# Two decode layers on one core: the whole first W_q kept in SBUF, a shorter ring, and a layer's first queries and scores head by head

## The chip, the cores and the metric

One Trainium2 chip, one of its cores. The metric is the device time of one execution of the program in microseconds. Before the change the median of three runs is 736.22 us (736.16 to 736.47).

## What is computed

Four sequences (B = 4) decode one token through two equal layers, each an attention block and a gated MLP with a residual around either. All arrays are float32. Both layers use the same weights and the same cache, of which the last W = 1024 positions count.

```python
def _A_ref(x, k_cache, v_cache, wq, wo):            # D = 640, 32 heads of 128, W = 1024
    q = (x @ wq).reshape(B, Sq, Hq, Dh).transpose(0, 2, 1, 3)
    k = k_cache[:, :, Sk - W:, :]; v = v_cache[:, :, Sk - W:, :]
    p = softmax(einsum("bhqd,bhkd->bhqk", q, k) * Dh ** -0.5)
    return einsum("bhqk,bhkd->bhqd", p, v).transpose(0, 2, 1, 3).reshape(B, Sq, Hq * Dh) @ wo

def _B_ref(x, W_gate, W_up, W_down):                # F = 1728
    gate = x @ W_gate
    return (gate * (gate > 0) * (x @ W_up)) @ W_down

x = x + _A_ref(layernorm(x), ...); x = x + _B_ref(layernorm(x), ...)   # twice
```

## The kernel before

All that is loaded lies in three arrays of 128 partitions, cut along the free axis. `heads` holds W_q, keys, values and W_o of heads 0 to 26 in the order in which layer 0 uses them. `kept` holds the same for heads 27 to 31, and the MLP's weights are `mlp`. A head's keys are 4096 floats per partition, its values another 4096 and its W_o 640; W_q of a group of four heads is 2560. Heads are taken in groups: 0 to 5 have four heads each and 6 has three, all of them in `heads`; 7 (K0) has three and 8 (K1) two, and these are the kept ones. In layer 0 the order is all groups in turn; in layer 1 the kept groups come first, from what is still in SBUF.

Nearly all of SBUF is one tile, `store`, of 53888 floats per partition. Loads go into it as a ring: `load` walks through a list `todo` of pieces and puts each at the place `at`, which then moves on by the piece's length and goes back to 0 at the end. A piece of `kept` has a fixed place instead, its own offset in its row: W_o at 0 to 3200, the queries of the kept groups at 3200 to 6400, then keys and values up to 47360 (`FRONT`). While these stay, from the end of layer 0's attention through its MLP, the ring is what is left of the store, 47360 to 53888, 6528 floats. `jumps` sets the place where a new stretch begins.

`load` is called while the program is written, after each product that has read its operand for the last time (`done`), and emits a load only when the places that it overwrites have been read. So the order of all loads is fixed, all of them stand on SP's queue one behind the other, and each waits there for the PE instruction that read its place last. A piece longer than 16384 ends where a quarter of the store ends. The first `HELD` = 1024 floats of `heads`, a part of W_q of group 0, are loaded once into a tile of their own, `first_q`, and serve both layers.

On PE, a group goes through `query` (5 chunks of W_q), `query_out` (scaling, on DVE), `query_turned` (transposes), `scores` (8 products of 512 columns per head: two halves of the positions for each of four sequences), `softmax`, `turned`, `values` (8 products of 512 columns per head) and `project`. The products with the values of a group come after the scores of the next one. A product in float32 is two PE instructions in the profile, and one row entry in the order of instructions shown further down. In `attention` the first two groups' queries are computed ahead of the first group's scores. In `forward`, `gate` multiplies by W_gate and W_up, `down` by W_down, 640 floats of it at a time; `busy` issues transposes into `po` whose results nobody reads. All schedules are written by hand: each engine takes its instructions in the order in which the code emits them.

Of the kernel before, what the change touches and what calls it, by code (L numbers as in the profile page):

```python
# [7 lines left out]
F32 = mybir.dt.float32  # L8
AF = mybir.ActivationFunctionType
ALU = mybir.AluOpType  # L10
# [3 lines left out]
P = 128  # L14
# [13 lines left out]
SIDE = 4  # L28
# [5 lines left out]
def of(what, g):  # L34
    return [(what, h) for h in HEADS[g]]


def step(g):
# [7 lines left out]
    "kept": [*of("o", K0), *of("o", K1), ("q", K0), ("q", K1), *of("k", K0), *of("k", K1), *of("v", K0), *of("v", K1)],  # L46
# [44 lines left out]
def decode_kernel(ctx: ExitStack, tc: tile.TileContext, x, source, sel, out):  # L91
# [3 lines left out]
    small = ctx.enter_context(tc.tile_pool(name="small", bufs=2))  # L95
# [6 lines left out]
    big.tile([P, 8], F32, name="pad")  # L102
# [37 lines left out]
    pieces(1, "heads", HELD, 2560, 3584, k, *range(k + 1536, k + 4 * 1536 + 1, 1536))  # L140
# [16 lines left out]
    def load(part=False):  # L157
# [4 lines left out]
        while todo:  # L162
# [69 lines left out]
    qT = const.tile([P, SIDE - 1 + SIDE * SIDE * B], F32, name="qT")  # L232
# [9 lines left out]
    eps_sb = const.tile([P, 1], F32, name="eps_sb")  # L242
# [28 lines left out]
    def normalized():  # L271
# [3 lines left out]
        su = small.tile([P, 1], F32, name="su", bufs=1)  # L275
# [5 lines left out]
        ss = small.tile([P, 1], F32, name="ss", bufs=1)  # L281
        nc.scalar.activation(sq, xc, AF.Square, accum_out=ss)
        busy(1)

# [6 lines left out]
        return ss  # L291

    def deviation(ss):
        var = mean(ss, "var")
        rs = small.tile([P, 1], F32, name="rstd")
        nc.scalar.activation(rs, var, AF.Sqrt, bias=eps_sb)
        nc.vector.reciprocal(rs, rs)
        return rs

    def table(func):  # L300

        t = small.tile([P, 1], F32, name="t", bufs=1)
        nc.scalar.activation(t, eps_sb, func)
# [7 lines left out]
    def query(layer, g, spread=False):  # L311


        n = len(HEADS[g]) * P
        qp[g] = ps_m.tile([P, n], F32, tag="m", name="qp")
        for c in range(KC - 1):
            nc.tensor.matmul(qp[g][32 * c:32 * c + 32, :], xT[:, B * c:B * c + 32], part(layer, "q", g, c * n, n),  # L317
                             start=True, stop=c > 0 and not spread, tile_position=(0, 32 * c))
        c = KC - 1
        m = n // 4 if spread else n  # L320
        for a in range(n // m):
            nc.tensor.matmul(qp[g][32 * a:32 * a + 32, a * m:a * m + m], xT[:, B * c:B * c + 32],  # L322
                             part(layer, "q", g, c * n + a * m, m), start=False, stop=True, tile_position=(0, 32 * a))
        part_done(layer, "q", g, 0, KC * n)

    def query_out(g, rstd):
        nc.vector.tensor_scalar(gates[:, :len(HEADS[g]) * P], qp.pop(g), rstd, SCALE, op0=ALU.mult, op1=ALU.mult)  # L327

    def query_turned(g):

        n = len(HEADS[g])
        qt = ps_m.tile([P, n, P], F32, tag="m", name="qt")
        for i in range(n):
            nc.tensor.transpose(qt[:, i], gates[:, i * P:(i + 1) * P], ident)  # L334

        at = qT[:, SIDE - 1:].rearrange("p (i b x) -> p i b x", i=SIDE, b=B)[:, :n, :, 0]
        nc.vector.tensor_reduce(at, qt.rearrange("p i (a x) -> p i x a", a=4)[:, :, :B], axis=AX.X, op=ALU.add)

    def scores(layer, g):
        n = len(HEADS[g])  # L340
        for i, h in enumerate(HEADS[g]):
            for j in range(2):
                for b in range(B):
                    lo = (j * B + b) * 512
                    at = SIDE - 1 + SIDE * (B * i + b) - i
                    nc.tensor.matmul(ps[32 * b:32 * b + SIDE, j, :], qT[:, at:at + SIDE], part(layer, "k", h, lo, 512),  # L346
                                     start=i == 0, stop=i == n - 1, tile_position=(0, 32 * b))
                    part_done(layer, "k", h, lo, 512)
        nm[g] = small.tile([P, 1], F32, name="nm")
        nc.vector.tensor_reduce(nm[g], ps.rearrange("p j n -> p (j n)"), axis=AX.X, op=ALU.max, negate=True)  # L350

    def softmax(g):
        sums[g] = small.tile([P, 1], F32, name="sm")
        nc.scalar.activation(probs, ps.rearrange("p j n -> p (j n)"), AF.Exp, bias=nm.pop(g), accum_out=sums[g])  # L354
# [28 lines left out]
    def totals(g):  # L383
        so = ps_m.tile([P, P], F32, tag="m", name="so")
        nc.tensor.transpose(so, sums.pop(g).to_broadcast([P, P]), ident)  # L385
        r[g] = small.tile([P, SIDE, B], F32, name="r")
        nc.vector.reciprocal(r[g], so.rearrange("p (b i) -> p i b", b=B)[:, :SIDE])  # L387

    def values_turned(g):
# [5 lines left out]
        oT[g] = small.tile([P, SIDE, B], F32, name="oT")  # L395
# [12 lines left out]
    def attention(layer):  # L408
        gs = order[layer]
        load(True)  # L410
        rstd = deviation(normalized())
# [34 lines left out]
    def forward(layer):  # L446
        load(True)
        ss = normalized()
# [26 lines left out]
        def hidden(j, h):  # L475
            hTs[j] = small.tile([P, 4, B], F32, name="hT", bufs=4)
# [11 lines left out]
        def down(j, last=False):  # L488
            for f in range(4 if j < 3 else 1):
# [6 lines left out]
                if not (last and f > 1):  # L496
                    busy(1)
# [10 lines left out]
        rstd = deviation(ss)  # L508
# [75 lines left out]
```

## Time and profile before

| | us |
|---|---|
| median of three runs | 736.22 (736.16 to 736.47) |
| the profiled execution | 736.33 |
| its span, first to last instruction | 734.46 |
| PE busy | 452.5 |
| DVE busy | 75.0 |
| ACT busy | 47.1 |
| HBM read | 312.24 MB |

The profile is of one execution. Its page lists busy times, and behind it stand views in the order of time: an engine's instructions, SP's issues and, for each load, the time from its issue to its landing. A product of 128 partitions by 512 columns has a long time of its own in a row's mean (700 ns), but four of them run side by side in different columns of the array, so a stretch of them is read from its start and its length. Rows of one line, engine and shape are merged with an "x" and their number.

### The profile page before, as it was taken

The numbers are of one execution on the slowest core, as the hardware profiler recorded it, in microseconds if no ns is written. First come the engines' busy times: TensorE is split into PE (matmuls) and PEld (weight loads), VectorE is DVE, ScalarE is ACT, GpSimd is POOL, SyncE is SP. The second block draws the span as 40 slices with busy tenths as digits, with TensorE's granted clock in tenths as the row PEclk, the third lists the DMA queues.
The fourth block names the chain that finished last, engine by engine and source line by source line (L and its number), as shares of the span: only waits on it lengthen the run. The fifth ranks groups of instructions, "written<-read, shape, count | busy, mean of one in ns | idle before, by whom it ended". The sixth has DMA issues, their size and how long they took to land.

```text
span 734.5 us, 8243 instructions
## 1 busy us (share of the span) xinstructions
PE 452.5 (62%) x3749; PEld 142.7 (19%) x3749; DVE 75.0 (10%) x279; ACT 47.1 (6%) x88; POOL 0.2 (0%) x4
## 2 busy tenths in 40 slices
PE   1657366555566635727789897446756545656686
PEld 0111111111121201202233231101211111122242
DVE  1011010010000101101101221001010100001010
ACT  1100000000000000000101110000000000000110
POOL 0000000000000000000000000000000000000000
PEclk9989787867678887969899999867878977668897
DMA  9999999999999999999999999999999999999996
GB/s 380 454 421 430 452 430 422 429 446 434 417 444 445 408 446 419 438 433 419 419 405 406 432 433 431 445 432 443 431 427 425 447 432 424 435 445 429 420 427 285
DMA packets 15738, 312.85 MB, mean 426 GB/s; under 512 B 1748, under 2 KB 2132, under 8 KB 7512
## 3 DMA queue, kind: packets, MB, share of 16 engines
q1 hardware_dynamic: 15552, 312.24, 99.1%
q8 instruction: 29, 0.48, 0.2%
q10 hardware_dynamic: 152, 0.09, 0.1%
q14 instruction: 5, 0.04, 0.0%
HBM read 312.24 MB, written 0.08 MB: 425 GB/s over the span
## 4 chain that ended last, share of the span: by engine, by line
DMA 54%; PE 30%; another core or an unknown queue 14%; issue 1%; DVE 1%; ACT 0%; SPq 0%; DVEq 0%; ACTq 0%
DMA store<-in_heads 32%; PE ps L346 12%; DMA store<-in_mlp 12%; DMA store<-in_kept 10%; PE po L374 9%; PE y L404 1%; PE qp L317 1%; PE pp L359 1%; PE qp L322 1%; PE gu L458 1%; PE qt L334 1%; PE ot L394 0%; PE po L259 0%; PE y L493 0%
## 5 line engine op out<-in xcount | busy, mean ns | idle before, releaser
L346 PE MATMUL ps<-store,qT 128*4 128x512 f32 x1024 | 160.9, 700 | 108.2 <-DMA store<-in_heads 104.3
L374 PE MATMUL po<-store,pT 128*16 128x512 f32 x1024 | 155.2, 718 | 105.4 <-DMA store<-in_heads 95.4
L374 PEld LDWEIGHTS po<-store,pT 128*16 128x16 f32 x1024 | 35.0, 110 | 210.8 <-issue 128.3
L346 PEld LDWEIGHTS ps<-store,qT 128*4 128x4 f32 x1024 | 29.4, 94 | 221.6 <-DMA store<-in_heads 119.9
L350 DVE TENSOR_REDUCE nm<-ps 128x1 f32<-128x1024 f32 x18 | 22.0, 1224 | 245.0 <-PE ps L346 245.0
L354 ACT ACTIVATE probs<-ps,nm 128x1024 f32<-128x1024 f32 x18 | 20.1, 1114 | 353.6 <-DVE nm L350 345.9
L317 PE MATMUL qp<-store,xT 128*32 128x512 f32 (+2 forms) x136 | 22.9, 614 | 24.7 <-DMA store<-in_heads 24.6
L404 PE MATMUL y<-store,oT 128*4 128x160 f32 x512 | 26.2, 335 | 8.7 <-DMA store<-in_heads 7.6
L458 PE MATMUL gu<-store,xT 128*32 128x256 f32 (+1 forms) x300 | 26.3, 414 | 8.3 <-DMA store<-in_mlp 7.9
L370 DVE COPY pT<-pp 128x16 f32<-128x16 f32 x128 | 17.1, 168 | 135.3 <-PE po L374 135.3
L381 ACT COPY gates<-po 128x512 f32<-128x512 f32 x16 | 9.4, 587 | 243.1 <-PE po L374 243.1
L359 PE MATMUL pp<-sel_sb,probs 128*128 128x128 f32 x144 | 19.5, 281 | 0.0
L322 PE MATMUL qp<-store,xT 128*32 128x512 f32 (+4 forms) x48 | 17.7, 514 | 0.0
L327 DVE TENSOR_SCALAR gates<-qp,rstd 128x512 f32<-128x512 f32 (+2 forms) x18 | 12.4, 691 | 48.4 <-PE qp L322 44.4
L359 PEld LDWEIGHTS pp<-sel_sb,probs 128*128 128x128 f32 x144 | 17.1, 146 | 0.0
L404 PEld LDWEIGHTS y<-store,oT 128*4 128x4 f32 x512 | 13.3, 93 | 19.5 <-DMA store<-in_heads 8.0
L387 DVE RECIPROCAL r<-so 128x16 f32<-128x16 f32 x18 | 4.6, 257 | 121.4 <-PE so L385 121.4
L458 PEld LDWEIGHTS gu<-store,xT 128*32 128x32 f32 x300 | 11.4, 123 | 18.9 <-issue 8.7
L394 PE MATMUL ot<-sel_sb,gates 128*128 128x128 f32 x72 | 11.7, 283 | 1.2 <-DVE gates L378 1.2
L334 PE MATMUL qt<-sel_sb,gates 128*128 128x128 f32 x64 | 12.3, 316 | 0.0
L493 PE MATMUL y<-store,hT 128*4 128x160 f32 x208 | 10.6, 305 | 1.7 <-DMA store<-in_mlp 1.7
L334 PEld LDWEIGHTS qt<-sel_sb,gates 128*128 128x128 f32 x64 | 7.6, 155 | 18.8 <-issue 17.5
(62 smaller groups left out, 107.2 us busy)
## 6 DMA issues: line engine op xcount, KB each, us to landing
store<-in_heads SPq DMA_DIRECT2D x18, 6656.0 KB, 54.0
store<-in_heads SPq DMA_DIRECT2D x7, 6912.0 KB, 52.0
store<-in_heads SPq DMA_DIRECT2D x2, 6592.0 KB, 54.4
store<-in_heads SPq DMA_DIRECT2D x2, 5376.0 KB, 65.4
store<-in_mlp SPq DMA_DIRECT2D x16, 640.0 KB, 6.9
store<-in_kept SPq DMA_DIRECT2D x4, 2048.0 KB, 39.9
store<-in_heads SPq DMA_DIRECT2D x3, 2560.0 KB, 22.0
store<-in_heads SPq DMA_DIRECT2D x1, 6896.0 KB, 46.1
```

The lines of the kernel that those rows point to most:

```text
L317: nc.tensor.matmul(qp[g][32 * c:32 * c + 32, :], xT[:, B * c:B * c + 32], part(layer, "q", g, c * n, n), start=True, stop=c > 0 and not sp ...
L322: nc.tensor.matmul(qp[g][32 * a:32 * a + 32, a * m:a * m + m], xT[:, B * c:B * c + 32], part(layer, "q", g, c * n + a * m, m), start=False ...
L327: nc.vector.tensor_scalar(gates[:, :len(HEADS[g]) * P], qp.pop(g), rstd, SCALE, op0=ALU.mult, op1=ALU.mult)
L334: nc.tensor.transpose(qt[:, i], gates[:, i * P:(i + 1) * P], ident)
L346: nc.tensor.matmul(ps[32 * b:32 * b + SIDE, j, :], qT[:, at:at + SIDE], part(layer, "k", h, lo, 512), start=i == 0, stop=i == n - 1, tile_ ...
L350: nc.vector.tensor_reduce(nm[g], ps.rearrange("p j n -> p (j n)"), axis=AX.X, op=ALU.max, negate=True)
L354: nc.scalar.activation(probs, ps.rearrange("p j n -> p (j n)"), AF.Exp, bias=nm.pop(g), accum_out=sums[g])
L359: nc.tensor.transpose(pps[g][c // 4][:, c % 4, :], probs[:, c * P:(c + 1) * P], ident)
L370: nc.vector.tensor_copy(to[:, 4 * j:4 * j + 4], pp[j][:, :, i:P:32])
L374: nc.tensor.matmul(po[32 * a:32 * a + SIDE * B, :], t[:, at:at + SIDE * B], part(layer, "v", h, c * 512, 512), start=i == 0 and c < 4, sto ...
L404: nc.tensor.matmul(y[32 * a:32 * a + B], o[:, i], part(layer, "o", h, a * QUARTER, QUARTER), start=False, stop=last and h == HEADS[g][-1], ...
L458: nc.tensor.matmul(gus[j][32 * g:32 * g + 32, :2 * n], xT[:, B * c:B * c + 32], get(layer, "mlp", lo, 2 * n), start=c == 0, stop=c == KC - ...
```

## The change

Six things are changed. The whole W_q of group 0 (`HELD` = 2560) is kept in `first_q`. The store shrinks to 52480 floats, so the ring beside the kept rows has 5120. A quarter's end is now at multiples of 13312. The queries of the two kept groups change places in `kept`, and layer 1's first loads go to `LATER` (4480), from where the first kept group's queries and its keys follow each other. In `attention` the first group's queries are multiplied head by head (`query_by_heads`), its scores too, and the second group's queries come behind them. In `down`, two unread transposes stand behind every second block of W_down in place of one behind each. Small tiles that had buffers of their own now lie in spare columns of `qT`'s buffer or share one pool.

```diff
-    "kept": [*of("o", K0), *of("o", K1), ("q", K0), ("q", K1), *of("k", K0), ...
+    "kept": [*of("o", K0), *of("o", K1), ("q", K1), ("q", K0), *of("k", K0), ...
...
-HELD = 1024
-STORE = 53888
-QUARTERS = [STORE // 4, STORE // 2, STORE // 4 * 3, STORE]
+HELD = KC * 4 * P
+STORE = 55040 - HELD
+QUARTERS = [13312, 2 * 13312, 3 * 13312, STORE]
 FRONT = KEPT * 2 * (D + KV)
-FIRST, FIRST_MLP = 10944, 53248
+LATER = (KEPT + len(HEADS[K1])) * D
+FIRST, FIRST_MLP = 10752, STORE - 640
...
-    pieces(1, "heads", HELD, 2560, 3584, k, *range(k + 1536, k + 4 * 1536 + 1, 1536))
+    pieces(1, "heads", HELD, 3584, k, *range(k + 1536, k + 4 * 1536 + 1, 1536))
...
-                at = FRONT if layer == 0 and row == "mlp" else KEPT * D if layer == 1 and spare else 0
+                at = FRONT if layer == 0 and row == "mlp" else LATER if layer == 1 and spare else 0
...
+    def query_by_heads(layer, g):
+        n = len(HEADS[g]) * P
+        qp[g] = ps_m.tile([P, n], F32, tag="m", name="qp")
+        for i in range(len(HEADS[g])):
+            for c in range(KC):
+                a = c if c < 4 else i
+                nc.tensor.matmul(qp[g][32 * a:32 * a + 32, i * P:i * P + P], xT[:, B * c:B * c + 32],
+                                 part(layer, "q", g, c * n + i * P, P), start=c < 4, stop=c != i, tile_position=(0, 32 * a))
+        part_done(layer, "q", g, 0, KC * n)
...
-        query(layer, gs[0], True)
-        query_out(gs[0], rstd)
-        query(layer, gs[1])
-        query_turned(gs[0])
-        go_on()
-        query_out(gs[1], rstd)
-        scores(layer, gs[0])
-        softmax(gs[0])
+        g, n = gs[0], len(HEADS[gs[0]])
+        query_by_heads(layer, g)
+        query_out(g, rstd, 0, 1)
+        query_out(g, rstd, 1, 2)
+        query_turned(g, 0, 1)
+        query_out(g, rstd, 2, n)
+        go_on()
+        head_scores(layer, g, 0)
+        query_turned(g, 1, n)
+        for i in range(1, n):
+            head_scores(layer, g, i)
+        query(layer, gs[1])
+        highest(g)
+        query_out(gs[1], rstd)
+        softmax(g)
         query_turned(gs[1])
...
-                if not (last and f > 1):
-                    busy(1)
+                if j == 3 or f == 1 or f == 3 and not last:
+                    busy(2)
```

Since the ring is shorter and begins elsewhere, the pieces end at other floats and lie at other places. Around layer 0's turn to the kept rows the lists read so (floats of the row, places in the store, and the last read that frees them). Keys of head 24, the first behind the turn, begin at float 207744 of `heads`; values of head 19 fill 203648 to 207744, in 8 blocks of 512.

| before | place | behind | after | place | behind |
|---|---|---|---|---|---|
| heads 191360 to 204672 | 40320 to 53632 | keys of head 19 | heads 188288 to 200576 | 39808 to 52096 | keys of head 19 |
| heads 204672 to 207744 | 0 to 3072 | W_o of head 11 | heads 200576 to 207744 | 0 to 7168 | values of head 12 |
| kept 3200 to 6400 | 3200 to 6400 | values of head 12 | kept 3200 to 6400 | 3200 to 6400 | 7th value block of head 19 |
| heads 207744 to 214400 | 6400 to 13056 | values of head 14 | heads 207744 to 214400 | 6400 to 13056 | 8th value block of head 19 |
| heads 214400 to 228224 | 13056 to 26880 | keys of head 21 | heads 214400 to 227712 | 13056 to 26368 | (long read) |
| heads 228224 to 238976 | 26880 to 37632 | keys of head 23 | heads 227712 to 238976 | 26368 to 37632 | (long read) |

On SP these are the following rows, first before the change, with the semaphores on which each waits. DMAHW names the semaphores of earlier loads, PE that of PE's instructions.

```order
L186 DMA store<-in_heads 128x13312 [waits PE_49]
L186 DMA store<-in_heads 128x3072 [waits DMAHW0_49,PE_49]
L186 DMA store<-in_kept 128x3200 [waits PE_49]
L186 DMA store<-in_heads 128x6656 [waits PE_49]
L186 DMA store<-in_heads 128x13824 [waits DMAHW2_49,DMAHW1_49,PE_49]
L186 DMA store<-in_heads 128x10752 [waits PE_49]
```

The same place of SP's queue after the change:

```order
L187 DMA store<-in_heads 128x12288 [waits DMAHW7_49,PE_49]
L187 DMA store<-in_heads 128x7168 [waits DMAHW0_49,PE_49]
L187 DMA store<-in_kept 128x3200 [waits DMAHW4_49,PE_49]
L187 DMA store<-in_heads 128x6656 [waits PE_49]
L187 DMA store<-in_heads 128x13312 [waits DMAHW1_49]
L187 DMA store<-in_heads 128x11264 [waits DMAHW2_49]
```

The last piece ahead of the kept queries has 7168 floats where it had 3072, and the two long pieces behind them no longer wait for PE themselves.

The second place is PE's order where layer 1 begins: from the layer norm's variance to the second group's turned queries, before the change.

```order
L268 MATMUL var<-ss,sel_sb 32x1 x4
L317 MATMUL qp<-store,xT 32x384 x4
L322 MATMUL qp<-store,xT 32x96 x4
L317 MATMUL qp<-store,xT 32x256 x4
L322 MATMUL qp<-store,xT 32x256
L334 MATMUL qt<-sel_sb,gates 128x128 x3
L307 MATMUL y<-probs,sel_sb 128x160
L346 MATMUL ps<-store,qT 4x512 x24
L334 MATMUL qt<-sel_sb,gates 128x128 x2
```

And after it:

```order
L273 MATMUL var<-qT,sel_sb 32x1 x4
L329 MATMUL qp<-store,xT 32x128 x15
L342 MATMUL qt<-sel_sb,gates 128x128
L308 MATMUL y<-probs,sel_sb 128x160
L353 MATMUL ps<-store,qT 4x512 x8
L342 MATMUL qt<-sel_sb,gates 128x128 x2
L353 MATMUL ps<-store,qT 4x512 x16
L318 MATMUL qp<-store,xT 32x256 x5
L342 MATMUL qt<-sel_sb,gates 128x128 x2
```

The first group's queries are 15 short products instead of 8 longer ones, the first head's scores stand ahead of the turning of the other two heads, and the second group's queries have moved behind all scores of the first.

More of the change, by code (lines that the diff above doesn't have):

```diff
@@ L309, in decode_kernel, with query @@
     qp, nm, sums, pps, r, oT = {}, {}, {}, {}, {}, {}
-    def query(layer, g, spread=False):
+    def query(layer, g):
         n = len(HEADS[g]) * P
         qp[g] = ps_m.tile([P, n], F32, tag="m", name="qp")
[L316 to L323, printed above, removed]
-        part_done(layer, "q", g, 0, KC * n)
@@ L339, in scores @@
-    def scores(layer, g):
[L340 to L349, printed above, removed]
+        for c in range(KC):
+            a = c % 4
+            nc.tensor.matmul(qp[g][32 * a:32 * a + 32, :], xT[:, B * c:B * c + 32], part(layer, "q", g, c * n, n),
+                             start=c < 4, stop=a > 0 or c == 4, tile_position=(0, 32 * a))
@@ L447, in forward @@
         load(True)
-        ss = normalized()
+        normalized()
         gus, hTs = {}, {}
```

70 lines of the change are left out of this document (44 added, 26 removed).

## The prediction

> **What bounds the kernel now.** First the page: its busy shares, its DMA queues, and then the busy time by stretch. In the second fence the columns are engine busy times, the granted clock, the busy share of the 16 DMA engines and what they moved.
>
> ```profile
> span 734.5 us, 8243 instructions
> PE 452.5 (62%) x3749; PEld 142.7 (19%) x3749; DVE 75.0 (10%) x279; ACT 47.1 (6%) x88; POOL 0.2 (0%) x4
> q1 hardware_dynamic: 15552, 312.24, 99.1%
> HBM read 312.24 MB, written 0.08 MB: 425 GB/s over the span
> ```
>
> ```profile
> 12.00:250.00 238.00, 136.41 (x986) 37.98 (x990) 21.83 (x74) 13.32 (x23) 0.00 (x0) 0.80 1.00 432
> 366.00:392.00 26.00, 22.45 (x256) 9.29 (x256) 2.09 (x10) 1.97 (x7) 0.00 (x0) 1.00 1.02 404
> 396.00:450.00 54.00, 49.89 (x483) 16.87 (x482) 12.01 (x34) 7.25 (x14) 0.00 (x0) 1.00 1.02 430
> 725.00:734.00 9.00, 5.47 (x114) 2.44 (x113) 0.93 (x4) 0.15 (x1) 0.00 (x0) 0.88 0.43 169
> ```
>
> The transfers are the bound: SP's queue keeps 16 engines busy for 99.1% of the span, at 432 GB/s with large pieces and 404 GB/s in layer 0's MLP with small ones, and no stretch before the last 9 us shows a gap. PE is busy for 62%, but for 49.89 of 54 us where layer 1 begins. Two things follow. A microsecond of transfer saved is a microsecond off the end. And a microsecond in which the queue is empty is lost, because nothing later has slack to win it back. So I ask of every part whether it takes bytes away, and whether SP ever has to wait until everything issued has landed.
>
> **The change part by part. Bytes.** W_q of head group 0 stays in SBUF whole, so layer 1 loads 1,536 floats per partition fewer: 1,536 x 512 B = 0.786 MB, at 432 GB/s **1.8 us less**. SP also issues two pieces fewer (the rows of its order: 105 against 107 loads through SP). A 640 KB piece is 0.655 MB, 1.62 us at 404 GB/s and 1.52 at 432, so an issue costs about 0.1 us: **0.2 us less**.
>
> **The turn to the kept rows in layer 0.** This is where I expect the time. Before, SP issues the queries of the kept heads early:
>
> ```profile
> 204.01 0.33 SPq L186 DMA_DIRECT2D store<-in_heads  x1
> 205.71 0.33 SPq L186 DMA_DIRECT2D store<-in_kept  x1
> 208.30 30.07 SPq L186 DMA_DIRECT2D store<-in_heads  x3
> store<-in_kept SPq DMA_DIRECT2D x1, 1600.0 KB, 48.4
> ```
>
> That piece is issued at 205.71 and lands 48.4 us later: 48 us of transfers lie ahead of it. Its place is fixed, 3200 to 6400. In the table of the change the piece of `heads` in front of it ended at place 3072; now it ends at 7168, and covers 3200 to 6400 with the values of head 19 from float 128 to 3328. The kept queries can start only when PE has read the seventh of head 19's eight blocks, and those blocks are in the piece issued immediately ahead. SP takes its queue in order, so behind this wait stand 6,656, 13,312 and 11,264 floats of `heads`; the order's rows show that the last two wait for no PE instruction of their own. So the queue runs dry: the piece lands, PE multiplies, and only then the next transfer starts. PE's rows there (start, length):
>
> ```profile
> 238.41 1.27 PE L404 MATMUL y<-store,oT 128*4 128x160 f32 x32
> 246.83 9.32 PE L374 MATMUL po<-store,pT 128*16 128x512 f32 x64 [7.15 <-DMA store<-in_heads]
> 262.01 5.10 PE L346 MATMUL ps<-store,qT 128*4 128x512 f32 x26 [2.90 <-DMA store<-in_heads]
> 119.54 8.09 PE po L374 x44
> 68.71 6.19 PE po L374 x52
> out_x<-probs SPq DMA_DIRECT2D x1, 80.0 KB, 1.6
> first_q<-in_heads SPq DMA_DIRECT2D x1, 512.0 KB, 3.9
> ```
>
> When does the piece land? At 246.83 PE starts on the piece that ends at float 204,672. 3,072 floats more are 1.573 MB, 3.6 us: 250.4. The way back from 262.01 agrees: that wait ended when the 3,200 kept floats and the 6,656 of `heads` had landed, 5.05 MB or 11.7 us later, so 250.3. The bytes up to float 207,744 are the same in the change, so this moment stays. What has PE left then? The last piece holds 14 value blocks (6 of head 18, 8 of head 19). The piece ahead ends at 200,576, 4,096 floats or 4.9 us before 204,672, so it lands at about 241.9. After its last key block come the query turn, the projection (1.27 us) and 18 value blocks at 9.32/32 = 0.291 us (two instructions to a block), 5.2 us: PE is done at about 249.2 and waits. Then 13 blocks, **3.8 us**, until the kept queries may go. Bounds: 6.19/26 = 0.238 us a block gives 3.1, 8.09/22 = 0.368 gives 4.8.
>
> From that issue to a moving stream again costs what an issue into an empty queue takes beyond its bytes. Two rows bound it. The output's 80 KB took 1.6 us, 0.2 of it bytes: 1.4. The first load's 512 KB took 3.9 us, 1.2 of it bytes: 2.7, in the cold first microseconds. I take **1.5**, next to the output, which like this one goes out in a program long under way. Together the stream stands still for **5.3 us** (4.5 to 7.5). Late next are the keys of head 24, for which PE waits at 262.01 already, so all after them moves by as much.
>
> On this restart the Trainium skill's page "DMA: Bandwidth & Descriptors" (section "Anatomy of one DMA — SWDGE (gpsimd) path") fits a fixed cost of about 2.0 us to one transfer, for a path that this kernel does not use. By it the standstill would be 5.8 us and the time, as an estimate, 740.8. The rows, 1.4 and 2.7, lie on both sides of it.
>
> **The smaller ring.** In layer 0's MLP the ring has 5,120 floats instead of 6,528. The first of these rows is from 370 to 375 us, the second from 385 to 390:
>
> ```profile
> store<-in_mlp SPq DMA_DIRECT2D x3, 640.0 KB, 6.9
> store<-in_mlp SPq DMA_DIRECT2D x3, 640.0 KB, 5.9
> 371.25 2.23 PE L458 MATMUL gu<-store,xT 128*32 128x256 f32 x20 [0.49 <-DMA store<-in_mlp]
> ```
>
> One turn of the ring at 404 GB/s now takes 8.3 us (3.34 MB), and 6.5 in the change (2.62 MB). In a turn a piece lands, PE reads it, SP issues its successor and that lands: 1.6 us for its 640 KB and 1.4 to 2.7 beyond them. That leaves PE 2.2 to 3.5 us to read a piece; 20 instructions, two pieces, took 2.23. So the 6.9 and 5.9 us were mostly queue, the turn still closes, and I put the MLP at **nothing**. It is tighter where layer 1 begins, since between the last W_down block and the first queries PE frees no place:
>
> ```profile
> 396.94 0.39 SPq L186 DMA_DIRECT2D store<-in_heads  x1
> store<-in_heads SPq DMA_DIRECT2D x1, 256.0 KB, 7.0
> 398.76 0.85 PE L317 MATMUL qp<-store,xT 128*32 128x384 f32 x8
> 399.66 6.61 SPq L186 DMA_DIRECT2D store<-in_heads  x6
> 401.40 5.33 PE L346 MATMUL ps<-store,qT 128*4 128x512 f32 x48
> 366.70 1.18 PE L458 MATMUL gu<-store,xT 128*32 128x128 f32 x27 [0.30 <-DVE xT L290]
> ```
>
> The piece issued at 396.94 lands 7.0 us later, at 403.9, and is the last one until 399.66, when the queries of group 7, layer 1's first, are read: 4.2 us of transfers lie ahead. In the change the ring holds 1,408 floats less, 1.7 us at 430 GB/s, so it would be empty at 402.2. The queries by heads are 15 products, 30 instructions; of that form 27 took 1.18, so 1.3 us against 1.0 now, and the issue comes at about 400.0, 2.2 us ahead: enough. It frees only 512 floats, 0.6 us, so the queue lasts to 402.8. The next piece waits for the first key block. One head's queries are copied and turned sooner than three, which about pays for the longer product, so the scores start as now at 401.4; four blocks run side by side in 4 x 0.22 us (48 instructions, 24 blocks, in 5.33), so its release is near 402.2. At 1.5 us beyond the bytes the stream resumes 0.9 us late. After that each block frees its place in 0.22 us and is refilled in 0.6, so nothing more is lost. **0.8 us** (0 if the first block is free at its own end, 2.0 at 2.7 beyond the bytes).
>
> **The rest costs nothing.** Head by head adds 7 products to group 7's queries and 12 to group 0's; the second queries come after the scores; the products that nobody reads are one more in number, in pairs. All of it is PE work, and what hides it is the transfers: elsewhere PE waits for them, as the rows of waits above show. The places where PE sets SP's pace are costed already. Without that cover the query's extra instructions would cost 0.3 us. The small tiles that move into one buffer change no row that I can price.
>
> **The sum.** The profiled execution took 736.3 us, 1.8 outside its span of 734.5; the median of the three runs is 736.2, so nothing is lost by starting there. 736.2 - 1.8 - 0.2 + 5.3 + 0.8 = **740.3 us**. With every bound low it is 736.2 - 2.0 + 4.5 + 0 = 738.7, with every bound high 736.2 - 1.8 + 7.5 + 2.0 = 743.9.
>
> **The rivals.** *The kept queries do not wait for head 19.* Then the wait in their row would be for the earlier contents of that place, and they would go out near 206 us as before. For it: the order's row names PE, not the instruction. Against it: the places in the table overlap, and head 19's blocks have to be read before they are overwritten. Then 736.2 - 2.0 + 0.8 = 735.0, and 734.2 if layer 1's start loses nothing: faster. What decides is the issue of the 1,600 KB piece: before the piece ahead lands at 250.4, or after.
>
> *The ring is too small throughout.* If a transfer needs 2.7 us beyond its bytes and PE 2.7 to read a piece with its unread products, a turn takes 7.0 us instead of 6.5. The MLP's 25,920 floats are five turns: 2.5 us more, with 2.0 in place of 0.8 at layer 1: 744.0. For it: the 5.9 us between issue and landing late in the MLP, near one small turn. Against it: the engines' share of 1.02 there, which shows no gap in a ring that has only 1.8 us more.
>
> *The standstill is partly paid by the engines' own lag.* In the last 9 us the 16 engines move 169 GB/s: they end at different times, and the slowest ends the kernel. A common restart at 256 us takes away what lag they have by then. That gives back up to about 2 us: 738.3. For it: 1.52 MB in those 9 us would take 3.5 at full rate. Against it: the slowest engine loses the standstill too, and its lag can come after it.
>
> **How the numbers follow.** The forecast, a dry queue at 250 us, has 0.80; the engines' lag 0.08, the small ring 0.06, no wait at the kept queries 0.06. The first two hold 738.2 to 743.0, with the corner of all high bounds left out; the small ring lies above and the missing wait below. Slower by over 0.2% (1.5 us, about what a measurement of this kernel can tell from no change) means over 737.7: 0.92, the first three cases but for 0.02 at the lag's edge. Faster means below 734.7: of the missing wait's 0.06 I give it 0.04, since its two times lie on both sides of that line. Within 0.2%: 0.04, half from the missing wait and half from the lag.
>
> **What would show it.** In the profile after, the 1,600 KB piece of `kept` is issued at about 254 us and lands some 5 us later instead of 48; the slice of the DMA row there falls well below the 9 it has everywhere; the three `heads` issues behind it follow within 2 us. HBM reads 311.45 MB. Around 402 us the transfers show a gap of about 1 us, in the MLP none. I am wrong if that issue stays near 206 us, if PE has more than 14 blocks left when the piece lands (each 0.3 us more), or if the MLP's rate falls well below 404 GB/s.

## The result, and the profile after

The kernel after the change takes 748.27 us (median of 5 runs, 747.82 to 749.85) against 736.22 (736.16 to 736.47): ratio 1.0167, 95% interval 1.0153 to 1.0181. It is slower, as forecast, but by 12.05 us where I had 4.1, and outside my range. The profiled executions took 747.82 and 736.33, so 11.49 us are to be found in the trace.

The page of the kernel after (in the DMA and GB/s rows a slice is 18.7 us, so the fourteenth is 242 to 261 us and the twenty-first to twenty-third are 373 to 429):

```profile
span 746.0 us, 8327 instructions
PE 457.8 (61%) x3788; PEld 143.1 (19%) x3788; DVE 76.1 (10%) x285; ACT 47.1 (6%) x88; POOL 0.2 (0%) x4
DMA  9999999999999699999999999999999999999996
GB/s 385 443 420 457 418 434 442 420 440 436 426 437 422 270 457 415 427 441 419 419 381 348 365 436 429 440 441 437 432 425 443 435 420 444 432 426 431 426 428 286
q1 hardware_dynamic: 15264, 311.45, 97.8%
HBM read 311.45 MB, written 0.08 MB: 418 GB/s over the span
```

The bytes fell as forecast, and the span grew: the same queue works at 97.8% of a longer span. Two dents are new. One slice has 270 GB/s, and three in a row have 381, 348 and 365. The busy time by stretch shows what is in them (granted clock, DMA share and GB/s are the last three columns):

```profile
250.00:254.00 4.00, 4.00 (x38) 1.22 (x33) 0.17 (x1) 0.00 (x1) 0.00 (x0) 1.00 0.00 0
376.00:406.00 30.00, 21.27 (x242) 8.63 (x243) 1.47 (x7) 1.10 (x3) 0.00 (x0) 1.00 0.97 359
402.00:412.00 10.00, 7.38 (x127) 4.02 (x123) 2.03 (x8) 2.47 (x6) 0.00 (x0) 0.95 0.99 392
412.00:416.00 4.00, 3.71 (x22) 0.62 (x18) 0.19 (x1) 0.00 (x0) 0.00 (x0) 0.71 0.54 154
416.00:462.00 46.00, 43.45 (x397) 14.38 (x393) 10.16 (x28) 4.79 (x8) 0.00 (x0) 1.00 1.01 432
737.00:746.00 9.00, 4.14 (x97) 2.02 (x85) 0.50 (x2) 0.00 (x0) 0.00 (x0) 0.97 0.36 144
```

There are three holes. For 4 us at 250 nothing moves at all; through the 30 us of layer 0's MLP the rate is 359 GB/s where it was 404; for 4 us where layer 1 begins it is 154. After 416 us the rate is 432, where the row of before has 430. In the MLP the engines' busy share is 0.97 where it was 1.02, 5% less, for a rate that is 11% lower, so a share near 1 does not show that the queue was full. The granted clock was 1.00 there, so a slower PE clock does not explain this second hole. How much each costs is told by landings: the moment at which the last of the 16 engines finished a piece, in us from the start of the span.

| landing of | before | after | later by | lost since the row above |
|---|---|---|---|---|
| the piece ahead of the kept queries | 250.33 | 250.21 | -0.1 | |
| the kept queries | 254.10 | 260.21 | 6.1 | 6.2 |
| the last kept piece | 364.19 | 370.58 | 6.4 | 0.3 |
| the last piece of layer 0's MLP | 396.17 | 406.70 | 10.5 | 4.1 |
| layer 1's heads up to float 50,176 | 455.75 | 467.15 | 11.4 | 0.9 (2.7 lost, 1.8 of bytes saved) |
| the last piece | 730.94 | 742.38 | 11.4 | 0.0 |

The first hole is the standstill that I forecast. SP's issues and PE's instructions around it (start, length), and from the view of the loads the time from issue to landing:

```profile
202.22 0.33 SPq L187 DMA_DIRECT2D store<-in_heads  x1
253.89 0.33 SPq L187 DMA_DIRECT2D store<-in_kept  x1
254.27 1.42 SPq L187 DMA_DIRECT2D store<-in_heads  x3
```

```profile
246.51 7.36 PE L388 MATMUL po<-store,pT 128*16 128x512 f32 x64
260.35 2.39 PE L318 MATMUL qp<-store,xT 128*32 128x384 f32 x10 [4.92 <-DMA store<-in_kept]
```

```profile
store<-in_kept SPq DMA_DIRECT2D x1, 1600.0 KB, 6.3
```

The piece of the kept queries goes out at 253.89 instead of 205.71, at the end of PE's run of value blocks (246.51 + 7.36 = 253.87), and lands 6.3 us later instead of 48.4, with the next three issues close behind. From 250.21 to 253.89 the queue is empty: 3.7 us. The piece's 1.638 MB take 3.8 us at 432 GB/s, so 2.5 of its 6.3 us are beyond the bytes. Afterwards PE waits for it, 4.92 us.

### The profile page after: what moved, and what is told of

The parts are those of the page before. It is cut to its first block, busy times and chain, and to the rows that moved or that the text cites. A ratio compares the mean times of both kernels' runs of the same rounds, so it can differ in the third digit from the quotient of the medians.

```text
span 746.0 us, 8327 instructions
## 1 busy us (share of the span) xinstructions
PE 457.8 (61%) x3788; PEld 143.1 (19%) x3788; DVE 76.1 (10%) x285; ACT 47.1 (6%) x88; POOL 0.2 (0%) x4
## 3 DMA queue, kind: packets, MB, share of 16 engines
q1 hardware_dynamic: 15264, 311.45, 97.8%
HBM read 311.45 MB, written 0.08 MB: 418 GB/s over the span
## 4 chain that ended last, share of the span: by engine, by line
DMA 44%; PE 36%; another core or an unknown queue 17%; DVE 1%; issue 1%; SPq 0%; ACT 0%; DVEq 0%; ACTq 0%
DMA store<-in_heads 30%; PE ps L353 15%; PE po L388 11%; DMA store<-in_kept 9%; DMA store<-in_mlp 6%; PE qp L318 3%; PE y L418 2%; PE pp L373 1%; PE qt L342 1%; PE gu L480 1%; PE ot L408 0%; SPq L187 0%; PE so L399 0%; PE y L515 0%
## 5 line engine op out<-in xcount | busy, mean ns | idle before, releaser
L353 PE MATMUL ps<-store,qT 128*4 128x512 f32 x1024 | 170.6, 741 | 118.0 <-DMA store<-in_heads 112.8
L388 PE MATMUL po<-store,pT 128*16 128x512 f32 x1024 | 152.2, 696 | 93.4 <-DMA store<-in_heads 84.0
L318 PE MATMUL qp<-store,xT 128*32 128x512 f32 (+2 forms) x150 | 31.7, 653 | 28.4 <-DMA store<-in_heads 23.4
L364 DVE TENSOR_REDUCE qT<-ps 128x1 f32<-128x1024 f32 x18 | 22.0, 1225 | 249.8 <-PE ps L353 249.8
L368 ACT ACTIVATE probs<-ps,qT 128x1024 f32<-128x1024 f32 x18 | 20.1, 1115 | 378.2 <-DVE qT L364 378.2
L418 PE MATMUL y<-store,oT 128*4 128x160 f32 x512 | 23.5, 320 | 14.4 <-DMA store<-in_heads 13.2
L335 DVE TENSOR_SCALAR gates<-qp,qT 128x512 f32<-128x512 f32 (+3 forms) x22 | 13.1, 603 | 56.2 <-PE qp L318 52.7
L318 PEld LDWEIGHTS qp<-store,xT 128*32 128x32 f32 x150 | 6.1, 118 | 41.1 <-DMA store<-in_heads 27.1
## 6 DMA issues: line engine op xcount, KB each, us to landing
store<-in_heads SPq DMA_DIRECT2D x3, 2560.0 KB, 18.7
```

The costliest lines, as they stand in the source:

```text
L318: nc.tensor.matmul(qp[g][32 * a:32 * a + 32, :], xT[:, B * c:B * c + 32], part(layer, "q", g, c * n, n), start=c < 4, stop=a > 0 or c == 4 ...
L335: nc.vector.tensor_scalar(gates[:, at], qp[g][:, at], rstd, SCALE, op0=ALU.mult, op1=ALU.mult)
L388: nc.tensor.matmul(po[32 * a:32 * a + SIDE * B, :], t[:, at:at + SIDE * B], part(layer, "v", h, c * 512, 512), start=i == 0 and c < 4, sto ...
L418: nc.tensor.matmul(y[32 * a:32 * a + B], o[:, i], part(layer, "o", h, a * QUARTER, QUARTER), start=False, stop=last and h == HEADS[g][-1], ...
```

## The experiments

Three theories stood at the start. **A**: the three holes are separate losses, the standstill worth 6 and the ring of 5,120 floats worth the rest. **B**: the standstill is the cause of all, and the later holes follow from it, so that without it the kernel gains its 1.8 us. **C**: the ring is innocent, and the new order in which PE works (head by head, pairs of unread products) opens the holes. In every set of runs the kernel before ran beside the others on the same chip, with medians of 736.4 to 736.6 and single executions from 736.0 to 739.2.

**1. The turn free, the ring short.** The heads start at another place of the ring, so that the kept queries' place is not the one of head 19's values.

```diff
-FIRST, FIRST_MLP = 10752, STORE - 640
+FIRST, FIRST_MLP = 7168, STORE - 640
```

> The changed kernel with the ring's first place at 7168 instead of 10752, so that the piece ahead of the kept queries ends at place 3072 again; all else is the change. Theory A (three separate losses: 6.1 us standstill at the kept queries, 4.2 in the MLP from the ring of 5120, 2.8 where layer 1 begins; 2.0 gained): 748.3 - 6.1 = 742.2 us, the 1600 KB piece lands some 48 us after its issue, the MLP and the start of layer 1 still lose 4 and 3. Rival B (the standstill upsets the order of the transfers, and the later losses follow from it): 734 to 736.

742.25 us (741.95 to 743.35), ratio 1.0074, 1.0061 to 1.0087. The queue's issues and the landing of the kept piece in this kernel:

```profile
206.35 0.33 SPq L187 DMA_DIRECT2D store<-in_kept  x1
```

```profile
store<-in_kept SPq DMA_DIRECT2D x1, 1600.0 KB, 47.6
```

One number removes the standstill, and with it 6.0 of the 12.05 us. Theory B falls: the other 6 remain. Layer 0's MLP lands at 401.04, 4.9 us later than before.

**2. The ring long.** The change with only 1,024 floats of W_q kept, the ring of before, and its places.

```diff
-HELD = KC * 4 * P
-STORE = 55040 - HELD
-QUARTERS = [13312, 2 * 13312, 3 * 13312, STORE]
+HELD = 1024
+STORE = 53888
+QUARTERS = [STORE // 4, STORE // 2, STORE // 4 * 3, STORE]
-FIRST, FIRST_MLP = 10752, STORE - 640
+FIRST, FIRST_MLP = 10944, 53248
-    pieces(1, "heads", HELD, 3584, ...)
+    pieces(1, "heads", HELD, 2560, 3584, ...)
```

> The change with the sizes of before (1024 floats of W_q kept, store of 53888, ring of 6528, first places as before): what is left of the change is the order head by head, the unread products in pairs, the kept queries' order and the packed small tiles. Theory A: 736.2 us within 0.7, no loss in the MLP or at layer 1's start. Rival C (the new orders cost, not the sizes): 740 or more, with the losses of the change in the MLP and at layer 1's start.

738.58 us (736.51 to 742.67, 12 runs), ratio 1.0025, 1.0011 to 1.0039. Neither A's nor C's figure: nearly 10 of the 12 us are gone, but 2 are left, and the runs scatter by 6 us. Part of the rest lies outside the span from the first to the last instruction: 2.0 to 3.0 us in 8 of the 12 executions, where the kernel before has 1.7 to 1.9. The profiled execution was the slowest of them, and is looked at below.

**3. The ring short in the kernel before.** Nothing of the change but its ring; the kept queries go out early (205.55).

```diff
-STORE = 53888
+STORE = 52480
-FIRST, FIRST_MLP = 10944, 53248
+FIRST, FIRST_MLP = 5888, STORE - 640
```

> The kernel before with the store cut to 52480 floats, so the ring beside the kept rows has 5120, and the first place moved so that the kept queries do not collide; nothing else. Theory A: 736.2 + 4.2 + 2.8 = 743.2 us (742 to 745, since the first queries free less at a time), transfer engines idle in the MLP. Rivals B and C: 736 to 737.

745.29 us (743.13 to 748.12), ratio 1.0114, 1.0094 to 1.0135. The ring alone, with no other part of the change and no byte saved, costs 8.7 us at the median and 6.5 in its fastest run, which is the profiled one. The median lies just above A's 742 to 745, far from B's and C's 736 to 737: both fall. The MLP of its profiled execution lands at 401.13, again 5.0 us late; the rest is lost where layer 1 begins.

**4. A ring between the two.** 1,536 floats of W_q kept, a ring of 6,144.

```diff
-HELD = KC * 4 * P
+HELD = 1536
-FIRST, FIRST_MLP = 10752, STORE - 640
+FIRST, FIRST_MLP = 9984, STORE - 640
-    pieces(1, "heads", HELD, 3584, ...)
+    pieces(1, "heads", HELD, 2560, 3584, ...)
```

> The change with 1536 floats of W_q kept and a ring of 6144, free of the collision at the kept queries. Theory A: 0.6 us gained by bytes, and of the 7 us that the short ring loses the part that a ring 1024 longer leaves; if the loss grows evenly from a ring of 6528, 736.2 - 0.6 + 7 x 384/1408 = 737.5; if there is a threshold between, 735.6. Rival C: 740 or more.

741.80 us (740.30 to 744.59), ratio 1.0067, 1.0050 to 1.0084: not what A expected. The trace shows why, and it is no verdict on the ring's length alone. In this ring the first piece of layer 1 falls on the place of the MLP's last block. SP's issues, the way of that piece, and the stretch:

```profile
391.07 1.62 SPq L187 DMA_DIRECT2D store<-in_mlp  x3
400.64 2.34 SPq L187 DMA_DIRECT2D store<-in_heads  x5
```

```profile
store<-in_heads SPq DMA_DIRECT2D x1, 512.0 KB, 3.8
```

```profile
397.00:401.00 4.00, 3.45 (x36) 1.39 (x36) 0.31 (x1) 0.00 (x0) 0.00 (x0) 0.57 0.12 46
```

I had made a second standstill: the MLP's last landing is at 398.96, the next issue at 400.64, the DMA share 0.12. As an accident it is useful. Its first piece, 512 KB or 1.2 us of bytes, landed 3.8 us after an issue into an empty queue: 2.6 beyond the bytes, the same as the 2.5 of the kept queries. The MLP in this ring landed 2.8 us late, between the -0.2 to 1.3 of the executions with 6,528 floats and the 4.9 of run 1 with 5,120.

**5 to 7 and 9 to 11. Order and products.** The 2 us of run 2 could be the head by head order or the pairs of unread products, so I undid them in the long ring and in the short one (with the turn free): the order by `query` and the calls of the kernel before, the products by one behind each block. Runs 5 and 6 undo one of the two in the long ring, run 9 both; runs 10, 11 and 7 do the same in the short one.

```diff
-        query_by_heads(layer, g)
...
-        head_scores(layer, g, 0)
-        query_turned(g, 1, n)
-        for i in range(1, n):
-            head_scores(layer, g, i)
-        query(layer, gs[1])
+        query(layer, gs[0], True)
+        query_out(gs[0], rstd)
+        query(layer, gs[1])
+        query_turned(gs[0])
...
+        scores(layer, gs[0])
...
-                if j == 3 or f == 1 or f == 3 and not last:
-                    busy(2)
+                if not (last and f > 1):
+                    busy(1)
```

> The run with the long ring (738.6, 2.4 above the kernel before, spread 736.5 to 742.7) with the unread products as before: one behind each W_down block of layer 0 instead of two behind every second. Theory P (the pairs leave PE idle long enough that the granted clock drops to 0.5 at layer 1's start, and this is what scatters the times): 736 to 737, no half-clock interval after 350 us, a narrow spread. Theory H (the head by head order costs the 2 us): 738 to 739 as before the edit. Theory R (neither: new packing or a rate that varies): 738 to 739 too, and the next run the same.

> The run with the long ring, with the first queries and scores of both layers in the order of before (all heads' queries, both groups' queries ahead of the scores), the pairs of unread products kept. Theory H: 736 to 737. Theories P and R: 738 to 739.

> The run with the turn free (742.3; ring of 5120, whole W_q kept, kept queries not held up) with both the order and the unread products of before. Theory A (the ring of 5120 alone sets it: about 4.5 us lost in layer 0's MLP and 2 to 3 at layer 1's start, less 1.8 for the bytes): 741 to 743, layer 0's MLP landed at 400.5 to 401.5. Theory H or P, if they act beside the ring: 739.5 to 740.5, 2 us less.

> The run with the long ring (738.6), with the first queries and scores and the unread products both as before: what is left of the change is the place of the kept queries and the packing of the small tiles. If head by head and pairs cost their 2 us together or one by one: 736.2 to 736.9, the kernel before. If the kept order or the packing costs it: 737.5 to 739.

> The run with the turn free (742.3, ring of 5120), with one unread product behind each W_down block as before, head by head kept. The run with both undone took 744.9. If the order (head by head) is what helps in the short ring: 742 to 743 here, and 744.5 to 746 in the next run. If the pairs help: 744.5 to 746 here.

> The run with the turn free (742.3, ring of 5120), with the first queries and scores in the order of before, the pairs kept. If head by head helps in the short ring: 744.5 to 746. If the pairs help: 742 to 743. If neither does and single executions differ by as much: both of these runs overlap with 742.3 and 744.9.

Median us, and the 95% interval of the ratio to the kernel before:

| | ring of 6,528 | ring of 5,120, turn free |
|---|---|---|
| order and pairs of the change | 738.58 (1.0011 to 1.0039) | 742.25 (1.0061 to 1.0087) |
| its order, products of before | 737.48 (1.0005 to 1.0023) | 745.47 (1.0088 to 1.0131) |
| order of before, its pairs | 737.17 (1.0002 to 1.0019) | 744.24 (1.0087 to 1.0123) |
| both as before | 737.17 (0.9997 to 1.0024) | 744.87 (1.0081 to 1.0118) |

In the long ring the four can't be told apart: every interval overlaps with its neighbours, and by the medians the two parts cost 1.4 us together. In the short ring the two together take 2 to 3 us less than each alone or neither, whose intervals overlap. So theory H, theory P and theory A's "741 to 743" for run 7 all missed. Of the later three, run 9 falls between its two ranges, run 10 into the one for the pairs and run 11 into none. These medians do not show that the new order and the pairs cost the 2 us, nor that they win some of the short ring's loss back: each column is made of three sets of runs on three chips, the right one's top row rests on four executions, and the fastest executions of the rows under it (741.29 to 742.49) are as fast.

One cost of the order does show, outside the span. In the seven kernels that work head by head, 18 of 50 executions have 2.0 us or more there, up to 3.2; in the six that keep the order of before and in the kernel before, none of 126 has more than 1.94. It adds some 0.4 us to the mean of run 2 and 0.3 to that of run 5, whose profiled execution has 3.2. What the time is spent on is open.

**8. A finer cut.** If the ring's turn does not close, more floats on the way behind the release should help: MLP pieces of 512 and 640 floats instead of 1,280.

```diff
-FIRST, FIRST_MLP = 10752, STORE - 640
+FIRST, FIRST_MLP = 7168, STORE - 640
-    pieces(0, "mlp", 0, 1152, *range(GU0, WD0 + 1, 1280), WD1, *range(WD1 + 2 * D, MLP - D, 2 * D), MLP - D, MLP)
+    pieces(0, "mlp", 0, 1152, *range(GU0, WD0 + 1, 512), WD1, *range(WD1 + D, MLP + 1, D))
```

> The run with the turn free (742.3), with layer 0's MLP cut into pieces of 512 floats (W_gate, W_up) and 640 (W_down) in place of 1280: the ring keeps its 5120 floats, but 4608 instead of 3840 floats are on the way behind the piece whose reading releases the next. Theory A1 (the ring's turn does not close: from a landing through PE's reading to the next landing takes longer than what is on the way): the MLP's loss of 4.9 us falls to 1 to 2.5, the run takes 738.5 to 740.5. Theory A2 (in the ring of 5120 the rate is lost to something a finer cut does not change, such as packets or PE's own pace): 742 or more, MLP landed at 401 as in the run with the turn free.

740.70 us (739.66 to 742.08), ratio 1.0050, 1.0037 to 1.0062, just beside A1's range and under the 742.25 of run 1 (whose interval it touches). The MLP landed at 399.82: 1.2 of its 4.9 us are won, where A1 expected at least 2.4 and A2 none, so neither holds as it was put. The loads of the MLP in run 1, from 374 to 380 and from 386 to 392 us, and of run 8 in the same two windows:

```profile
store<-in_mlp SPq DMA_DIRECT2D x3, 640.0 KB, 5.1
store<-in_mlp SPq DMA_DIRECT2D x4, 640.0 KB, 5.3
```

```profile
store<-in_mlp SPq DMA_DIRECT2D x8, 256.0 KB, 4.6
store<-in_mlp SPq DMA_DIRECT2D x7, 320.0 KB, 5.0
```

A piece of half the size needs nearly the same time to land. That is no fixed time of a transfer. When a piece of the first window is issued in run 1, two or three earlier ones have not landed yet, in run 8 seven: about the same number of floats, 3,400 and 3,200 on average. So the finer cut buys less than A1 expected from the floats that it adds, and the ring's length counts for more than its pieces.

**12. The clock by itself.** In the traces the granted clock falls to 0.5 in stretches of 3.4 us or a multiple where layer 1 begins, in some executions and not in others. (It does so again and again in the attention stages of every trace: the prediction's rows have 0.80 for layer 0's.) Here is run 2's slowest execution, and under it the last experiment: the kernel before, without the products that nobody reads.

```profile
397.00:404.00 7.00, 6.03 (x82) 3.31 (x85) 2.04 (x8) 2.47 (x6) 0.00 (x0) 0.53 0.96 356
404.00:408.00 4.00, 4.00 (x19) 0.64 (x18) 0.00 (x0) 0.00 (x0) 0.00 (x0) 0.54 0.63 183
```

```diff
-            for _ in range(n):
+            for _ in range(0):
```

> The kernel before, without the products that nobody reads (W_down of layer 0 and the layer norms); ring, order and bytes as before, the output the same. In the executions profiled so far, layer 1's start loses 0 to 1 us in a ring of 6,528 floats where the granted clock stays at 1.0, and 4.5 in the one where it was 0.5 for 10 us around it. Theory K (the half clock itself costs the time there, through slower releases): without these products PE idles more, the granted clock falls to 0.5 somewhere in 390 to 410, and the run takes 739 to 742 in a ring that is as long as before. Theory L (the half clock only goes along with a ring that has run dry, and costs nothing by itself): 736.0 to 737.0.

737.82 us (736.22 to 740.23), ratio 1.0016, 1.0004 to 1.0028. Its profiled execution, 737.14, and the kernel before in the same windows:

```profile
390.00:397.00 7.00, 3.61 (x77) 1.36 (x65) 0.50 (x2) 0.00 (x0) 0.00 (x0) 1.00 1.01 407
397.00:404.00 7.00, 6.26 (x60) 3.09 (x64) 1.88 (x6) 2.47 (x6) 0.00 (x0) 0.52 1.01 396
404.00:408.00 4.00, 4.00 (x44) 0.90 (x40) 0.00 (x0) 0.00 (x0) 0.00 (x0) 1.00 0.95 342
```

```profile
390.00:397.00 7.00, 6.45 (x91) 2.54 (x91) 0.35 (x2) 0.00 (x0) 0.00 (x0) 1.00 1.00 411
397.00:404.00 7.00, 6.51 (x86) 2.80 (x88) 2.03 (x7) 2.47 (x6) 0.00 (x0) 1.00 1.02 414
404.00:408.00 4.00, 3.11 (x30) 0.72 (x22) 1.20 (x2) 0.00 (x0) 0.00 (x0) 1.00 1.05 438
```

Without these products PE is busy for 3.61 of the 7 us ahead of layer 1 instead of 6.45, the clock is halved for the next 6.8, layer 1's first scores start at 403.64 instead of 401.40, and the rate falls to 342 GB/s once the ring has emptied. The row of these scores (the kernel before's stands in the prediction):

```profile
403.64 5.38 PE L346 MATMUL ps<-store,qT 128*4 128x512 f32 x48
```

The MLP's last landing is that of before (396.06 against 396.17), so the later scores come from PE. By the landings this costs 1.5 us at layer 1's start, in the long ring and with no byte changed; at the last piece the kernel is 0.9 us late. So in this execution the half clock is a cause (theory K's mechanism), but of 1.5 us, not of K's 3 to 6; L's 736 to 737 misses too, by 0.8.

With that the executions line up by ring and clock. The loss at layer 1's start (landing of float 50,176 against that of the MLP's end, both against before, with the saved bytes added back) and about how long the clock was at 0.5 between 390 and 415 us:

| execution | ring | at half clock | lost there |
|---|---|---|---|
| before; both as before, long (9); order of before, long (6) | 6,528 | 0; 3.4; 3.4 us | 0; 0.4; 0.3 us |
| products of before, long (5) | 6,528 | 0 | 1.1 |
| no unread products (12) | 6,528 | 6.8 | 1.5 |
| long ring (2) | 6,528 | 10 | 4.7 |
| after; turn free (1); finer cut (8); products of before (10) | 5,120 | 3.4 each | 2.7; 3.3; 2.9; 3.7 |
| short ring in the kernel before (3); order of before (11) | 5,120 | 6.8 each | 2.2; 3.3 |
| turn free, both as before (7) | 5,120 | 10 | 5.7 |

The two executions with 10 us at half clock lose most in their ring. The short ring loses 2 to 4 us there with 3.4 us of it and with 6.8. Run 4 is left out, since its own standstill lies there. One execution each is no proof. In runs 1, 3, 10 and 11 the clock was back at 1.0 before the first scores began and stayed there through them, and 3.3, 2.2, 3.7 and 3.3 us were lost all the same. In run 3, the clearest, it was back at 399.11, 2.0 us before the MLP's last landing:

```profile
400.00:410.00 10.00, 9.53 (x130) 4.12 (x130) 2.21 (x7) 2.47 (x6) 0.00 (x0) 1.00 0.97 361
```

So the short ring loses time here without half clock in the scores; the half clock ahead of them may still have delayed the first issues. No run took it away altogether from a kernel with the short ring, so how the change's 2.7 us divide between ring and clock stays open. So does what makes the clock fall in one execution and not in another.

No version beat the kernel before. The best with the whole W_q kept is run 8, 740.70.

## Why the prediction was off

**Right.** What bounds the kernel, and, in the change, that a standstill is not won back: the last two rows of the landings are both 11.4 late. In other kernels a little is: run 1 is 6.4 us late at float 50,176 and 5.6 at its last piece. The bytes (311.45 MB, 1.8 us). The place, cause and start of the standstill: the issue at 253.89 against "about 254", behind head 19's value blocks, and run 1 shows that moving the place alone takes 6.0 us away. The rivals without a wait and with the engines' lag giving back 2 us are out. The restart did draw the 16 engines together, to 0.6 us from first to last at the kept queries where they were 2.0 apart before. But at the last piece they were 3.5 us apart again (4.0 before), and the last 9 us move 144 GB/s, no more than before's 169.

**The step that failed** is the smaller ring: "So the 6.9 and 5.9 us were mostly queue, the turn still closes, and I put the MLP at nothing." It measured 4.1 us there (4.9 in run 1, 5.0 in run 3): the turn did not close. At 359 GB/s the ring's 2.62 MB took 7.3 us to go round instead of 6.5. The term that was mis-sized is a piece's way from issue to landing. I had priced it at 1.6 us of bytes and 1.4 to 2.7 beyond them, 3.0 to 4.3 together, as if nothing lay ahead of it. In the short ring the same 640 KB still took 5.1 to 5.3 us. With 1.1 to 2.2 us for PE's reading (2.2 was the row for two pieces) a turn is then 6.2 to 7.5 us long, and the ring holds 6.5.

Why the way stays that long while the rate falls is not shown. Queue is still a large part of it: when the pieces of run 1's two windows were issued, two or three earlier ones had yet to land, the last of them 2.7 to 4.6 us later, and a piece needs 1.6 us more for its own bytes. But four of these seven landed 1.8 to 2.7 us behind the one ahead of them instead of 1.6: that is the time lost. One candidate is that a landing is that of the slowest engine. The 16 engines lay 1.6 to 2.9 us apart over the same MLP in the kernel before already (first to last engine of a piece: 366.78 to 369.66, 394.61 to 396.17), so the fastest can run out of work while the slowest still has a queue. No run takes this spread away. I read an issue-to-landing time as slack that a shorter ring would give back, and it gave back less than 1 us of 5.9. The share of 1.02 in the MLP, which I used against the small ring, does not tell how long a ring has to be.

**Terms that were mis-sized.** The restart: 1.5, measured 2.5 (and 2.6 in run 4). I took the output's 80 KB as the nearest row; the first load's 2.7, which I set aside as cold, was the better one. The Trainium skill's fit of about 2.0 us to one transfer ("DMA: Bandwidth & Descriptors", section "Anatomy of one DMA — SWDGE (gpsimd) path") lies nearer than my 1.5 and still under both measurements, which decide. The wait ahead of it, 3.8 forecast and 3.7 measured, was right by two errors that cancel, which is luck: PE had not caught up at 249.2, as I thought, but was in the middle of 32 blocks at 0.23 us, with 16 left instead of 14. That is one of the signs of being wrong that I had named. The products ahead of these blocks ran at half clock until 247.0 (the projection took 2.32 us, not 1.27), while the row that gave me 0.291 us a block ran at half clock itself until 251.5. Layer 1's start: 0.8, at most 2.0; measured 2.7. In the profiled execution its first scores ran at half clock, which no row of before has there:

```profile
411.00:412.00 1.00, 1.00 (x7) 0.59 (x11) 0.45 (x3) 0.00 (x0) 0.00 (x0) 0.50 1.01 399
412.00:413.00 1.00, 1.00 (x8) 0.15 (x4) 0.00 (x0) 0.00 (x0) 0.00 (x0) 0.50 0.69 262
413.00:414.00 1.00, 1.00 (x8) 0.15 (x4) 0.00 (x0) 0.00 (x0) 0.00 (x0) 0.50 0.14 51
```

The releases of the ring hang on these scores, and the queue empties while they run. That the clock could be halved just where the ring depends on PE was in no term and no rival. Runs 1, 3, 10 and 11 show that half clock in the scores is not the whole of this term.

**The chances.** "The ring is too small throughout" had 0.06 and was the case that came, beside the forecast's standstill, which it contained. It gave 744.0 with 2.5 us in the MLP and 2.0 at layer 1; with what was measured (6.2, 0.3, 4.1, 2.7, less 1.8) the sum is 736.3 + 11.5 = 747.8, the profiled time. Its own evidence, "the 5.9 us between issue and landing late in the MLP, near one small turn", deserved more than the share of 1.02 that I set against it.

## What to carry to other kernels

Before a ring of buffers is shortened, compare its turn with the shortest issue-to-landing time in the profile plus the reader's time, and do not count on that time to shrink with the ring until a row shows it smaller: here 640 KB took 5.9 us in a ring of 6,528 floats and still 5.1 to 5.3 in one of 5,120, of which 1.6 are its own bytes. Where a kernel is bound by one in-order queue, look for every load whose place is still being read when its turn comes; one such place cost 6 us, and moving it was one number. And where a matmul engine frees the buffers, its idle time can have a second price, if it comes back at half clock: 1.5 us in run 12.

## What the runs showed of the hardware

- A load into a drained queue needed 2.5 and 2.6 us beyond its bytes (1,600 and 512 KB), against 1.4 for 80 KB of output and 2.7 for the first load of the program.
- Halving a piece hardly shortened its way: 640 KB took 5.1 to 5.3 us, 256 KB 4.6 in the same ring, with about as many floats on the way ahead of it.
- The 16 engines of one queue drift apart: 2.0 us at the kept queries, 2.9 at the last kept piece and 4.0 at the last piece of the kernel before. A standstill of the queue drew them together to 0.6.
- The clock went to 0.5 without a long gap on PE. In the kernel after, PE's longest idle time in the 25 us ahead of it was 1.84 us, and it was busy for 3.00 of the last 4:

```profile
401.46 0.73 PE L515 MATMUL y<-store,hT 128*4 128x160 f32 x16 [1.84 <-DMA store<-in_mlp]
```

```profile
407.00:411.00 4.00, 3.00 (x67) 1.93 (x60) 1.59 (x6) 2.47 (x6) 0.00 (x0) 0.99 1.00 394
```

The Trainium skill ("TensorE: Matmul & The Clock Gate", section "What's actually happening") names one idle window of about 3.4 us as the condition. The stretches at 0.5 here are indeed 3.4 us or multiples of it, but in twelve executions the longest idle time in the 25 us ahead of such a stretch was 0.6 to 2.3 us. Its section "A second HAM failure mode: psum-queue depth-cycling" tells of a kernel in which many short idle times were enough, and that is nearer to these traces: some busy share of a window may decide. Which share, these runs don't tell. The kernel before shows how little an idle time by itself says: PE has one of 2.3 us that ends at 409.38, as runs 6 and 9 have at 409.58 and 409.29, and only in these two does the clock fall there.
